# The last batch's output stored by pairs of units, from the ring of output buffers

## The chip, the cores and the metric

One core of one Trainium2 chip. The metric is the device time of one launch in microseconds, as the median of several runs; the profile is of one such execution, and its span is 1.7 to 2.5 us shorter than the time of that run. The records call an execution slow when it is over 1.5% above the fastest of its kernel. Ratios and differences are of fast runs alone.

## The reference

Attention through 32 inducing points, twice, and then a feed-forward layer with GELU over all tokens:

```python
B, N, m, C = (4, 12480, 32, 128)          # x: [4, 12480, 128] float32
def mab(q, kv):
    s = scale * (q @ kv.transpose(0, 2, 1))
    a = softmax(s)                        # with 1e-9 added to the sum
    return a @ kv
h = mab(inducing, x)                      # 32 x 128 per batch
y = mab(x, h).reshape(49920, 128)
out = gelu(y @ w_in) @ w_out              # 128 -> 2048 -> 128, float32 [49920, 128]
```

The input and the output are 25.6 MB each. That is what the kernel has to move, whatever else it does.

## The kernel before

Of the engines, PE multiplies matrices, DVE, ACT and POOL work on elements, and SP issues stores; 16 DMA engines move data between HBM and SBUF. A store is issued when SP hands it to its DMA queue, and it has landed when a semaphore tells that all its parts are written.

Each batch is cut into six units of 2048 tokens and a tail of 192. The first pass (A) loads x, transposes it and gathers the 32 inducing points. A short chain then makes one small matrix per batch. The second pass (B) makes the outputs unit by unit: four matmuls per unit leave 128 x 512 values each in PSUM, and DVE, or ACT, or ACT followed by POOL, scales them into a buffer in SBUF. SP stores from there. Loads are issued by POOL (the first by SP) and, where POOL issues them, converted to 16 bits on the way; stores are issued by SP.

```python
XBUFS = 6          # ring of input buffers, 8 KB a partition each (32 x 128 of 16 bits)
OBUFS = 3          # ring of output buffers, 16 KB a partition each (32 x 128 of 32 bits)
APART = 3          # from this batch on, each unit is stored alone
SPENT = (B - 3, 2) # this pair is written over a transposed input that is no longer read
...
class Unit:
    ...
        self.pair = idx // 2                                  # two units share a pair
        self.c_pair = 0 if self.tail else 16 * (idx % 2)      # this unit's half of it
...
    def b_inverse(bt, u):
        ...                       # reciprocal of the sums, then the choice of buffer
        if u.tail:
            o = sb.tile([TP, 2, 128], FP32, tag="ot", bufs=2)
        elif u.b >= APART:        # an input buffer, read as 32 bits: 16 x 128
            o = sb.tile([128, 32, 128], FP16, tag="xh", bufs=XBUFS)
            ...
        else:
            if u.first:
                if spent(u):
                    ...
                else:
                    pair = sb.tile([128, 32, 128], FP32, tag="o", bufs=OBUFS)
                bt.live[("pair", u.pair)] = pair
            o = bt.live[("pair", u.pair)][:, u.c_pair : u.c_pair + 16, :]
...
    def b_store(bt, u, alone):
        if alone:
            c0, c1, o = u.c_pair, u.c_pair + u.nc, bt.live[("o", u.idx)]
        else:
            c0, c1, o = 0, u.held, bt.live[("pair", u.pair)]
        nc.sync.dma_start(out=u.rows_of(out)[:, c0:c1, :], in_=o)
...
        alone = u.tail or u.b >= APART
        ...
        if u.last or alone:       # a pair is stored when its second unit is scaled
            stored = plan.add(key(6), {"SP": 0.4}, ...)
```

The order of all instructions comes from a list scheduler that the kernel runs while it is built. It knows the rings and an assumed duration of each piece; the order is then pinned for each engine.

Of the kernel before, what the change touches and what calls it, by code (L numbers as in the profile page):

```python
# [31 lines left out]
LOAD_US = 2.43  # L32
STORE_US = 2.47
LEAD = (0, 0, 0, 0)
APART = 3
SPENT = (B - 3, 2)
LANDED_US = 1.1
FIRST_US = {"POOL": 1.3, "SP": 0.8}
# [210 lines left out]
def kernel(  # L249
# [409 lines left out]
    def b_inverse(bt, u):  # L659
# [4 lines left out]
        if u.tail:  # L664
            o = sb.tile([TP, 2, 128], FP32, tag="ot", bufs=2)
        elif u.b >= APART:
            o = sb.tile([128, 32, 128], FP16, tag="xh", bufs=XBUFS)
# [214 lines left out]
    for k, u in enumerate(order):  # L882
# [24 lines left out]
        )  # L907
        alone = u.tail or u.b >= APART
        if alone:
# [382 lines left out]
```

## Time and profile before

| | |
|---|---|
| time | 133.07 us, median of 3 (132.73 to 133.23) |
| span of the profile | 131.5 us |
| PE, DVE, ACT, POOL busy | 77%, 70%, 59%, 50% of the span |
| HBM traffic | 27.67 MB read, 25.56 MB written, 405 GB/s over the span |

The page's DMA row gives, for each fortieth of the span, the share of time in which the 16 DMA engines moved something, in tenths; the GB/s row gives what they moved, counted in what was written. A load that halves the data on its way therefore counts half. Behind these rows stand the packet records of the trace: for each row of a transfer its start, duration, size and queue, but not its engine. How many of the 16 engines are busy is counted from them.

### The profile page before, as it was taken

The page shows a single profiled execution, that of the slowest core. Times are in us where ns is not written, and L with a number is a line of the kernel's source. Part 1 is how long each engine was busy: PE and PEld are TensorE (multiplying, and loading weights), DVE is VectorE, ACT ScalarE, POOL GpSimd, SP SyncE. Part 2 cuts the span into 40 slices and gives each one's busy share as a digit, 9 for nine tenths or more (in the row PEclk, how much of TensorE's full clock was granted, in tenths as well). Part 3 has the DMA queues.
Part 4 walks back from the last instruction along what each step waited for, and adds up shares of the span by engine and source line. Part 5 has one row for each costly group of instructions (what it writes and reads, how often), then busy time and mean ns, then how long its engine had stood idle before and what let it go on. Part 6 is the DMA issues. An engine that isn't in the chain of part 4 may idle for free. (4 is left out here: it accounts for less than half of the span.)

```text
span 131.5 us, 3505 instructions
## 1 busy us (share of the span) xinstructions
PE 101.8 (77%) x1365; PEld 60.0 (46%) x1365; DVE 91.9 (70%) x265; ACT 77.1 (59%) x177; POOL 65.6 (50%) x85
## 2 busy tenths in 40 slices
PE   0967789479999999999697699999999499781000
PEld 0255656278646557565362565735645312320000
DVE  1825447525899998999999367999899756997000
ACT  3006154426776879499787378889797457754000
POOL 7910131039634556894815367965269763483000
PEclk9999869855999999999999689999999856999555
DMA  5999999999999999999999999999999999999981
GB/s 152 298 228 209 217 198 219 218 214 222 214 209 214 214 229 339 306 387 368 322 304 339 277 251 297 316 401 411 439 425 415 419 444 419 411 426 424 431 349 43
DMA packets 5666, 40.17 MB, mean 305 GB/s; under 512 B 624, under 2 KB 1936, under 8 KB 2192
## 3 DMA queue, kind: packets, MB, share of 16 engines
q0 software_dynamic: 2848, 13.30, 49.9%
q1 hardware_dynamic: 2752, 26.61, 48.5%
q8 instruction: 11, 0.18, 0.5%
q10 hardware_dynamic: 48, 0.02, 0.1%
q14 instruction: 7, 0.06, 0.1%
HBM read 27.67 MB, written 25.56 MB: 405 GB/s over the span
## 5 line engine op out<-in xcount | busy, mean ns | idle before, releaser
L702 POOL TENSOR_TENSOR pair<-pair,rr 128x512 f32<-128x512 f32 x26 | 26.8, 1043 | 19.6 <-ACT pair L365 16.7
L686 PE MATMUL at<-q,e 128*128 128x512 f16 (+1 forms) x104 | 33.7, 391 | 3.6 <-DVE xT L363 1.2
L377 PE MATMUL tr<-identity_h,xh 128*128 128x128 f16 x392 | 32.7, 244 | 3.1 <-DMA xh<-in_x_dram 3.1
L377 PEld LDWEIGHTS <-xh 128*128 128x128 f16 x392 | 27.5, 111 | 9.2 <-DMA xh<-in_x_dram 4.2
L363 DVE COPY xT<-tr 128x1024 f16<-128x1024 f16 (+1 forms) x36 | 22.7, 646 | 10.1 <-PE tr L377 9.6
L365 ACT ACTIVATE xT<-tr 128x1024 f16<-128x1024 f16 (+1 forms) x16 | 15.7, 980 | 18.6 <-PE tr L377 18.5
L717 DVE TENSOR_TENSOR pair<-at,rr 128x512 f32<-128x512 f32 x36 | 23.3, 676 | 1.1 <-PE at L686 0.4
L287 POOL DMA_DIRECT2D xh<-in_x_dram x15 | 8.3, 555 | 21.3 <-DMA xh<-in_x_dram 10.5
L403 ACT ACTIVATE e<-s 128x512 f16<-128x512 f32 (+1 forms) x28 | 15.3, 546 | 5.7 <-PE s L391 5.4
L638 ACT ACTIVATE e<-s 128x512 f16<-128x512 f32 (+1 forms) x28 | 14.9, 562 | 3.4 <-PE s L626 1.8
L365 ACT ACTIVATE pair<-at 128x512 f32<-128x512 f32 x26 | 15.7, 602 | 1.1 <-PE at L686 1.0
L417 DVE STREAM_TRANSPOSE e1t<-e 128x256 int32<-128x256 int32 (+1 forms) x28 | 11.1, 399 | 3.4 <-ACT e L403 3.3
L686 PEld LDWEIGHTS <-e 128*128 128x128 f16 (+1 forms) x104 | 8.7, 103 | 10.2 <-issue 6.7
L425 PE MATMUL hun<-xh,e1t 128*32 128x128 f16 x392 | 10.8, 226 | 3.1 <-DVE e1t L417 3.0
L572 POOL TENSOR_TENSOR pt<-pt 128x512 f32<-128x512 f32 (+4 forms) x20 | 12.0, 602 | 2.1 <-DVE rr L661 0.7
L717 DVE TENSOR_TENSOR o<-at,rr 128x512 f32<-128x512 f32 (+1 forms) x19 | 10.5, 579 | 2.9 <-PE at L686 2.5
L391 PE MATMUL s<-xT,indT 128*32 128x512 f16 (+1 forms) x108 | 10.5, 379 | 1.4 <-DVE xT L363 0.8
L425 PEld LDWEIGHTS <-e1t 128*32 128x32 f16 x392 | 6.4, 98 | 8.9 <-DVE e1t L417 6.5
L626 PE MATMUL s<-xT,hT 128*32 128x512 f16 (+1 forms) x100 | 10.0, 407 | 0.5 <-DVE rr L661 0.5
L702 POOL TENSOR_TENSOR o<-o,rr 128x512 f32<-128x512 f32 x7 | 7.3, 1041 | 5.7 <-ACT o L365 3.3
L650 PEld LDWEIGHTS <-e 128*128 128x128 f16 (+1 forms) x104 | 5.7, 99 | 4.8 <-issue 1.9
L650 PE MATMUL r<-strand,e 128*128 128x4 f16 (+1 forms) x104 | 6.7, 168 | 0.2 <-ACT e L403 0.2
(76 smaller groups left out, 102.0 us busy)
## 6 DMA issues: line engine op xcount, KB each, us to landing
out_dram<-pair SPq DMA_DIRECT2D x8, 2048.0 KB, 15.0
xh<-in_x_dram POOLq DMA_DIRECT2D x11, 1024.0 KB, 28.2
out_dram<-o SPq DMA_DIRECT2D x6, 1024.0 KB, 8.8
out_dram<-spent SPq DMA_DIRECT2D x1, 2048.0 KB, 16.1
x_first<-in_x_dram SPq DMA_DIRECT2D x1, 1024.0 KB, 5.2
xh<-in_x_dram POOLq DMA_DIRECT2D x1, 512.0 KB, 6.9
w_in_h<-in_moe_w_in_dram POOLq DMA_DIRECT2D x1, 512.0 KB, 17.2
w_out_h<-in_moe_w_out_dram POOLq DMA_DIRECT2D x1, 512.0 KB, 19.2
```

The source lines that it names most:

```text
L363: nc.vector.tensor_copy(out=out, in_=in_)
L365: nc.scalar.activation(out=out, in_=in_, func=AF.Copy)
L377: nc.tensor.transpose(tr[:, c - c0, : u.p], xh[: u.p, c, :], identity_h[: u.p, : u.p])
L403: nc.scalar.activation(out=e1[: u.p, : u.nc // 2, :, :], in_=s1[: u.p, : u.nc, :].rearrange("r (a b) i -> r a i b", b=2), func=AF.Exp, sca ...
L417: nc.vector.transpose(out=pairs(e1t)[: u.p, :n], in_=pairs(e1)[: u.p, :n])
L425: nc.tensor.matmul(bt.hun[32 * j : 32 * j + 32, :], e1t[: u.p, c // 2, :, c % 2], xh[: u.p, c, :], start=u.idx == 0 and c < 4, stop=c + 4 ...
L572: nc.gpsimd.tensor_tensor(out=bt.pt[:, :, :, :half], in0=bt.pt[:, :, :, :half], in1=bt.pt[:, :, :, half : 2 * half], op=ALU.add,)
L638: nc.scalar.activation(out=e2[: u.rows, : u.cols], in_=s2[: u.rows, : u.cols], func=AF.Exp, scale=SCALE,)
L650: nc.tensor.matmul(r2[: u.p, ci, : u.nj], e2[: u.rows, ci * u.p : (ci + 1) * u.p], strand[: u.rows, : u.nj], start=True, stop=True,)
L686: nc.tensor.matmul(at[: u.p, : u.nj, :], e2[: u.rows, ci * u.p : (ci + 1) * u.p], bt.q[: u.rows, : u.nj, :], start=True, stop=True,)
L702: nc.gpsimd.tensor_tensor(out=part, in0=part, in1=rr2[: u.p, ci, : u.nj].unsqueeze(2).broadcast_to([u.p, u.nj, 128]), op=ALU.mult,)
L717: nc.vector.tensor_tensor(out=ov[: u.p, ci, :, :], in0=at[: u.p, : u.nj, :], in1=rr2[: u.p, ci, : u.nj].unsqueeze(2).broadcast_to([u.p, u. ...
```

## The change

The intent is to store all full units in the same way: pairs in rows of 16 KB a partition, from the ring of three output buffers, the last batch's too.

```diff
-APART = 3
+APART = 4
```

With four batches, numbered 0 to 3, no unit is then stored alone but the tails. In the last batch three stores of 2 MB take the place of six of 1 MB.

## The prediction

> **What bounds the kernel now.** I read the page's slices first, then the busy times by stretch, then the chain that ended last, then the DMA issues, and last the store line itself in narrow stretches. The slices and three rows of the page:
>
> ```profile
> span 131.5 us, 3505 instructions
> DVE  1825447525899998999999367999899756997000
> DMA  5999999999999999999999999999999999999981
> GB/s 152 298 228 209 217 198 219 218 214 222 214 209 214 214 229 339 306 387 368 322 304 339 277 251 297 316 401 411 439 425 415 419 444 419 411 426 424 431 349 43
> ...
> out_dram<-pair SPq DMA_DIRECT2D x8, 2048.0 KB, 15.0
> out_dram<-o SPq DMA_DIRECT2D x6, 1024.0 KB, 8.8
> ```
>
> One slice is 3.29 us. The compute engines are finished three slices before the end, the DMA engines almost at it, and from the 27th slice on the GB/s row stays at 401 to 444. So the last 43 us are one unbroken stream of output. The busy times by stretch say the same, with the row length in them (columns: stretch, length, busy time of PE, PEld, DVE, ACT, POOL, clock, DMA share, GB/s):
>
> ```profile
> 90.00:100.00 10.00, 9.70 (x117) 5.09 (x117) 9.46 (x26) 8.87 (x26) 5.64 (x6) 1.00 1.01 425
> 100.00:110.00 10.00, 7.81 (x74) 3.16 (x74) 7.09 (x21) 5.38 (x14) 6.99 (x10) 0.70 1.00 424
> 110.00:120.00 10.00, 7.47 (x48) 2.79 (x44) 9.36 (x32) 7.04 (x18) 5.80 (x6) 0.96 1.00 421
> ```
>
> Until about 112 us this stream is pairs of units (2 MB, rows of 16 KB); after it, single units (1 MB, rows of 8 KB). 425, 424 and 421 GB/s: the row length hardly shows.
>
> The chain of waits stops in the checks at the end of compute, because the profile cannot follow a landing back to its store. It is still useful, since its last piece gives the end of compute:
>
> ```profile
> 119.86 0.60 DVE hit L438 x8
> ...
> 120.95 0.14 DVE failed L979
> ```
>
> Compute is over at 121.1, 10.4 us before the end. What ends the run is the landing of the last stores. The store line in stretches that hold one issue each:
>
> ```profile
> L729 SPq DMA_DIRECT2D out_dram<-o x1: 333/333/333, 108.6 to 108.6; - x1
> DMA to landing us min/median/max: 9.1/9.1/9.1
> L729 SPq DMA_DIRECT2D out_dram<-o x1: 332/332/332, 111.8 to 111.8; - x1
> DMA to landing us min/median/max: 8.5/8.5/8.5
> L729 SPq DMA_DIRECT2D out_dram<-o x1: 332/332/332, 116.7 to 116.7; - x1
> DMA to landing us min/median/max: 8.5/8.5/8.5
> L729 SPq DMA_DIRECT2D out_dram<-o x1: 332/332/332, 119.8 to 119.8; - x1
> DMA to landing us min/median/max: 11.3/11.3/11.3
> L729 SPq DMA_DIRECT2D out_dram<-o x1: 1105/1105/1105, 120.2 to 120.2; - x1
> DMA to landing us min/median/max: 11.1/11.1/11.1
> ```
>
> These are units 0, 1, 3 and 5 of the last batch and its tail. Each waits 8 to 11 us in the queue though it moves for 2.5 us only. The tail lands at 120.2 + 11.1 = 131.3, and the span is 131.5: the stores end the run. Unit 0 lands at 117.7, unit 1 at 120.3, unit 3 at 125.2, unit 5 at 131.1.
>
> **What the Trainium skill says.** Page "DMA: Bandwidth & Descriptors", section "Bandwidth" (Measured): a 16 MB transfer runs at 425 GB/s, 97% of peak; the trace agrees, with 421 to 425 here. Its section "Queues, rings and completion order" says that on each DMA engine the descriptors of a row are taken in ring order, and its section "Why a DMA increments its semaphore by 16 and not by 1" that a transfer has landed only when all its engines have. The trace agrees: stores land in order of issue, and the slowest engine's share decides. Its section "Latency and other measured facts" puts the first byte of this path at about 0.6 us. The trace's nearest case is the first load: 5.2 us from issue to landing for 1 MB on idle engines, of which some 2.5 are transfer, so 2.7 us of fixed cost at both ends. I use the trace's number.
>
> **The change, part by part.** One constant. In the last batch the six full units no longer take a buffer of 8 KB a partition each out of the ring of six input buffers; three pairs of units take 16 KB a partition each from the ring of three output buffers, as the pairs of the other batches do, and three stores of 2 MB take the place of six of 1 MB. Nothing else moves: matmuls, exponentials, scalings and bytes are the same.
>
> (1) Removed: three issues on SP, 3 x 0.33 = 1.0 us, on an engine that otherwise waits. Worth 0 on the end.
>
> (2) Bytes per second. 6 x 1.05 MB = 6.3 MB at 421 GB/s is 14.9 us, at 425 it is 14.8. The packets themselves say the same: in the trace's packet records a piece of 8 KB takes 309 to 324 ns on one DMA engine and one of 16 KB 611 to 624. Worth 0 to -0.1 us. The longer rows buy nothing measurable.
>
> (3) Later issues. A pair can go only when its second unit is scaled. With the compute of before, the three issues stand where those of units 1, 3 and 5 stand now: 111.8, 116.7 and 119.8. The last one is unmoved, and so is the tail's. What matters is whether the queue runs dry before the first two. Ahead of pair 0 lie the last pair and the tail of batch 2. Their issues, 101.8 and 103.6, are 13.0 and 11.5 from landing, so the queue ahead is empty at 114.8 to 115.1 (slowest engine). Pair 0 issued at 111.8 has 3.3 us until then, against 2.7 of fixed cost (part of it at the far end, so needed less): no gap on the slowest engine. On the faster ones there is a gap: in the packet records the engines finish the 16 KB rows of batch 2 between 112.5 and 114.3, and a store issued at 111.8 starts by my estimate at 113.2 (the first load's first packet came 1.4 us after its issue), perhaps up to 2 us later under load. Faster engines have slack, since at the end they finish between 127.4 and 129.6, and the slowest only at 131.
>
> (4) Pair 0 then lands at 115.1 + 2 x 2.45 = 120.0 (2.45 us a MB from units 1 and 3: 125.2 - 120.3 = 4.9 for two). Pair 1 is issued at 116.7, again 3.3 us ahead: same margin. It lands at 124.9. Pair 2 is issued at 119.8 with 5 us in hand and lands at about 129.8; the same sum for before would give 115.1 + 6 x 2.45 = 129.8 against 131.1 measured, because the last stores on the slowest engine are slower (units 3 to 5 take 5.9 us and not 4.9; at 126.4 to 127 instruction fetches run there). I carry this 1.3 over: 131.1, tail 131.3. So +0 from this step, and +0.5 if the start under load takes 3.5 us instead of 1.4.
>
> (5) The output ring. Three buffers: pair 0 reuses that of batch 2's first pair, pair 1 the second's, pair 2 the third's. Those land at 104.6, 109.7 and 114.8 (issues 91.5, 98.5 and 101.8 plus 13.1, 11.1 and 13.0). First writes into units 0, 2 and 4 in the timeline of before: 106.1, 111.5 and about 116.1. Slack 1.5, 1.8 and 1.3 us: no wait if the order stays. In before these units wait for nothing either, because the input buffers have long been free.
>
> (6) The order of instructions comes from a list scheduler in the kernel, which will now see these three rings as taken and may put pieces of the last batch in another order. I cannot work that out from a profile; I allow 0 to +1 us, mean +0.3.
>
> Sum: -0.1 + 0 to 0.5 + 0.3, so 133.07 + 0.4, rounded: 133.5.
>
> **The rivals.** (a) Longer rows are faster and the change gains: for it speaks only 425 against 421; by 1% of 14.9 us it would make 132.9. Against it, the packet times. (b) The queue runs dry twice because a pair goes out later by one unit (3.2 us at pair 0: 108.6 to 111.8; 2.4 us at pair 1: 114.3 to 116.7), and nothing hides it: margin 0.6 us lost plus, say, 1.5 us of gap: 134.5 to 135. For it speaks that the backlog, 8 to 11 us for single units, shrinks to some 3 us. (c) The output ring becomes a wait: if the scheduler or slower landings push pair 1 or 2 back, each us of wait delays the issue and, since the margin of step 3 is spent, the end: 135 to 137. Against it: 1.3 to 1.8 us of slack at each of the three. (d) Compute gains by the freed input ring: no, nothing loads any more, 0.
>
> **Range and chances.** Most of the weight lies on steps 3 to 5, between 133.0 and 134.0; rival b and c make the upper tail. Range 132.7 to 135.2. Faster by over 2% (under 130.4) would need the stream to move 20% faster or start earlier: 1%. Slower by over 2% (over 135.7) needs rival c, or b in full: 8%. Within 2%: 91%.
>
> **What would show it.** Steps right: the GB/s row from 90 to 127 us without a slice under 400; three pair issues near 111.8, 116.7 and 119.8; waits of SP still on the scaling engines; landing of pair 0 about 8 us after issue, of pair 2 about 11; the span about 131.5 to 132. Step 3 wrong: a dip in the slices near 114 and 119, and landing of pair 0 after 120.5. Step 5 wrong: scalings of the last batch that wait for the landing of an output store. Step 6 wrong: the last scaling ends clearly later than 119.7. Step 2 wrong: over 430 GB/s after 115 us, and an earlier end.

## The result, and the profile after

| | before | after |
|---|---|---|
| time, median of 5 | 133.07 us (132.63 to 133.23) | 132.99 us (132.93 to 133.16) |
| span of the profile | 131.5 us | 131.1 us |

The ratio is 1.0004, with a 95% interval of 0.9982 to 1.0027: the same. (A ratio here is the mean time of one kernel's fast runs over the mean of the other's in the same rounds, so it is not quite the ratio of the medians.)

The stretches of after, with the same columns as those of before in the prediction (length, busy time of PE, PEld, DVE, ACT, POOL, clock, DMA share, GB/s):

```profile
90.00:100.00 10.00, 9.94 (x134) 5.36 (x131) 9.49 (x22) 7.94 (x20) 6.31 (x7) 1.00 1.01 427
100.00:110.00 10.00, 7.81 (x58) 2.71 (x55) 6.80 (x22) 5.52 (x13) 5.89 (x8) 0.66 1.01 429
110.00:120.00 10.00, 6.18 (x38) 2.34 (x37) 8.37 (x31) 7.00 (x20) 5.20 (x5) 0.95 1.01 429
```

The stream of stores has no hole. From 110 to 120 us it is 429 GB/s where it was 421; the 427 and 429 of the stretches ahead, whose rows are 16 KB in both kernels, differ by 2 and 5 from the 425 and 424 of before, so much of that is not the change; and from 116 to 126 us, where before moves single units alone, it is 429 against 426. In the packet records, all 16 engines are busy from 5 us to 126.7 us in both kernels.

The three pair stores of the last batch and its tail, one answer of the store line per issue (time of issue, and time from there to landing):

```profile
L729 SPq DMA_DIRECT2D out_dram<-pair x1: 332/332/332, 109.9 to 109.9; - x1
DMA to landing us min/median/max: 10.0/10.0/10.0
L729 SPq DMA_DIRECT2D out_dram<-pair x1: 332/332/332, 114.9 to 114.9; - x1
DMA to landing us min/median/max: 10.0/10.0/10.0
L729 SPq DMA_DIRECT2D out_dram<-pair x1: 333/333/333, 119.1 to 119.1; - x1
DMA to landing us min/median/max: 11.6/11.6/11.6
L729 SPq DMA_DIRECT2D out_dram<-o x1: 723/723/723, 119.5 to 119.5; - x1
DMA to landing us min/median/max: 11.4/11.4/11.4
```

So the pairs land at 119.9, 124.9 and 130.7 and the tail at 130.9. Units 1, 3 and 5 of before landed at 120.3, 125.2 and 131.1. The landings agree within half a microsecond, though these pairs were issued up to 2 us earlier than those units. The issues moved; the landings did not.

One thing is new. The chain that ended last goes through the landing of a store in after (start, length, what):

```profile
100.11 14.76 DMA out_dram<-pair
114.88 0.03 issue
114.90 0.05 DVEq L717
114.95 0.04 issue
115.00 0.69 DVE pair L717
```

The first scaling into the last batch's third pair waits until the store that empties its buffer has landed, at 114.9. The timeline has the same for the second pair:

```profile
110.12 0.60 ACT L365 ACTIVATE pair<-at 128x512 f32<-128x512 f32 x1 [0.35 <-DMA out_dram<-pair]
```

The ring of output buffers has become a wait in this execution, then, and the stream of stores has no hole from it. (In a second execution of the same program, below, the buffers came free 1.1 to 1.8 us before they were written.) The experiments ask why the time stands still: is it because nothing in the change has a cost, or because a gain and a loss cancel?

### The profile page after: what moved, and what is told of

Its sections match the earlier page's. It is cut to its first block, busy times and chain, and to the rows that moved or that the text cites. A ratio compares the mean times of both kernels' runs of the same rounds, so it can differ in the third digit from the quotient of the medians.

```text
span 131.1 us, 3497 instructions
## 1 busy us (share of the span) xinstructions
PE 100.7 (77%) x1365; PEld 59.2 (45%) x1365; DVE 91.6 (70%) x264; ACT 77.8 (59%) x181; POOL 65.5 (50%) x85
## 5 line engine op out<-in xcount | busy, mean ns | idle before, releaser
L702 POOL TENSOR_TENSOR pair<-pair,rr 128x512 f32<-128x512 f32 x33 | 34.1, 1040 | 26.5 <-ACT pair L365 20.4
L686 PE MATMUL at<-q,e 128*128 128x512 f16 (+1 forms) x104 | 33.1, 385 | 4.4 <-DVE xT L363 1.2
L717 DVE TENSOR_TENSOR pair<-at,rr 128x512 f32<-128x512 f32 x49 | 31.9, 679 | 4.7 <-PE at L686 2.9
L377 PE MATMUL tr<-identity_h,xh 128*128 128x128 f16 x392 | 31.4, 238 | 2.5 <-DMA xh<-in_x_dram 2.4
L377 PEld LDWEIGHTS <-xh 128*128 128x128 f16 x392 | 26.3, 108 | 8.8 <-DMA xh<-in_x_dram 3.8
L365 ACT ACTIVATE pair<-at 128x512 f32<-128x512 f32 x33 | 19.9, 603 | 5.9 <-PE at L686 4.4
L638 ACT ACTIVATE e<-s 128x512 f16<-128x512 f32 (+1 forms) x28 | 14.9, 562 | 3.2 <-PE s L626 1.8
L425 PE MATMUL hun<-xh,e1t 128*32 128x128 f16 x392 | 11.3, 235 | 3.0 <-DVE e1t L417 3.0
L710 ACT ACTIVATE pair<-at,rr 128x128 f32<-128x128 f32 x24 | 6.9, 382 | 0.9 <-DVE rr L661 0.9
L391 PEld LDWEIGHTS <-indT 128*32 128x32 f16 x108 | 3.5, 94 | 6.1 <-issue 3.2
```

The source lines that it names most:

```text
L365: nc.scalar.activation(out=out, in_=in_, func=AF.Copy)
L377: nc.tensor.transpose(tr[:, c - c0, : u.p], xh[: u.p, c, :], identity_h[: u.p, : u.p])
L391: nc.tensor.matmul(s1[32 * j : 32 * j + 32, : u.nc, :], indT, xT[:, :, 32 * j : 32 * j + 32], start=True, stop=True,)
L425: nc.tensor.matmul(bt.hun[32 * j : 32 * j + 32, :], e1t[: u.p, c // 2, :, c % 2], xh[: u.p, c, :], start=u.idx == 0 and c < 4, stop=c + 4 ...
L638: nc.scalar.activation(out=e2[: u.rows, : u.cols], in_=s2[: u.rows, : u.cols], func=AF.Exp, scale=SCALE,)
L686: nc.tensor.matmul(at[: u.p, : u.nj, :], e2[: u.rows, ci * u.p : (ci + 1) * u.p], bt.q[: u.rows, : u.nj, :], start=True, stop=True,)
```

## The experiments

The theory: the DMA engines are full to the end, so bytes set the time; the change keeps the bytes, and its later issues and ring waits stay inside what the queue ahead still holds. The rivals: (A) long rows gain and later issues lose, and the two cancel; (B) the ring costs time; (C) the stores are hidden whatever one does, so that something else ends the run. All edits are to the kernel after unless it is said. The edits are shown shortened. Each run was timed in 5 rounds beside the kernel before, whose median was 133.02 us beside four runs (each unit alone, two halves, the hold that was none, rows of 2 KB), 133.03 beside four (the two reversed orders, the store left out at the end, rows of 8 KB everywhere) and 133.28 beside the other four. Executions called slow: one of six with the second pair first, two of six with the third pair first and with either store left out.

### Same buffers, each unit stored as soon as it is done

```diff
+        if u.b == B - 1 and not u.tail:        # the unit's own half of the pair
+            c0, c1, o = u.c_pair, u.c_pair + u.nc, bt.live[("o", u.idx)]
         nc.sync.dma_start(out=u.rows_of(out)[:, c0:c1, :], in_=o)
...
-        if u.last or alone:
+        if u.last or alone or halved:          # halved: a full unit of the last batch
```

> The last batch writes into the pair buffers of the output ring, as in the kernel after, but each unit is stored alone as soon as it is done: 1 MB, rows of 8 KB. Theory (the 16 DMA engines are full to the end, bytes set the time, and both issue times leave the queue filled): 133.0, within 0.3 of before and after. Rival A (longer rows gain and later issues lose, and the two cancel): earlier issues without the ring of input buffers give nothing else, so 133.0 to 133.1 as well, but then the next run must be slower. Rival B (the ring of three costs time): 133.5 or more.

Measured: 132.99 us, ratio 0.9996 (0.9958 to 1.0034). Output buffers in place of input buffers, with the rows of before and each unit issued by itself (in this profile up to 1.7 us earlier than in before), make no difference.

### Same moment, short rows

```diff
-        nc.sync.dma_start(out=u.rows_of(out)[:, c0:c1, :], in_=o)
+        # last batch, full units: rows of 8 KB, two stores at the moment of one
+        for c in range(c0, c1, 16):
+            nc.sync.dma_start(out=u.rows_of(out)[:, c:c+16, :], in_=o[:, c-c0:c-c0+16, :])
```

> As after, at the same moment, but each pair of the last batch goes as two stores of 1 MB with rows of 8 KB. Only the row length differs from after. Theory: 133.0 to 133.2 (the packet records give 616 ns for 16 KB and 2 x 311 for twice 8 KB, 1% of 14.9 us = 0.15 us). Rival A (cancelling): 133.4 or more, as the gain of the long rows is gone and the later issue stays.

Measured: 133.06 us, ratio 0.9994 (0.9959 to 1.0029). The run is not slower than after, so there is no gain of the long rows for a loss to cancel, within the 0.3 to 0.4% that the interval allows. Rival A falls for a gain of 0.4 us or more; a smaller one this run can't exclude. The packet records of this run give 311 ns for a piece of 8 KB in the last stretch, those of after 616 for 16 KB: 1% between them, some 0.15 us of the 14.9, below what these runs can see.

### A hold that was none

```diff
+        if u.b == B - 1 and u.pair < 2 and not u.tail:
+            held.append((dst, o))
+            if u.pair < 1:
+                return
+            for dst, src in held:              # first pair, then second pair
+                nc.sync.dma_start(out=dst, in_=src)
+            return
```

> As after, but the store of the last batch's first pair is held back until its second pair is done, so its issue moves from about 109.9 to about 114.9 us, when the queue ahead of it empties (landing of the tail before it at 115.1 in the profile of after). Theory (issue times are free only as long as the queue ahead is not empty, with some 2.7 us of fixed cost per store): a gap of 1.4 to 2.5 us in the stream, 134.4 to 135.5. Rival C (stores at the end are hidden whatever their issue): 133.0.

Measured: 132.83 us, ratio 1.0000 (0.9948 to 1.0052). This is no evidence against the theory, because the edit did not do what it was meant to. The trace has the first pair's issue at 111.8, 5.0 us ahead of the second's at 116.8. Emitting an issue later in the program doesn't delay it: the two issues stand in SP's list in the same order, and each waits only for the writers of its own buffer. In the trace SP, DVE, ACT, POOL and PE do the same work in the same order as in after, so the run is a repetition of it.

As a repetition it is useful. In this execution the last pair of the batch before was issued at 102.1 us, in the profile of after at 100.1. Compute was 2 us later, and the spans are 131.0 and 131.1. The end does not follow compute. Nor is there a wait for the ring here: its buffers came free at 105.0, 109.9 and 114.7 us and were first written at 106.2, 111.6 and 115.8.

### The hold, made real: the second pair's store first

```diff
-            for dst, src in held:
+            for dst, src in [late[-1]] + late[:-1]:   # second pair, then first
```

> The hold that the third run was meant to be: in the last batch the store of the second pair is issued first and that of the first pair right after it, so that nothing of this batch is issued before about 114.9 to 116.8 us, while the queue ahead empties at about 115.1. Theory (an issue is free as long as it comes some 2 us before the queue ahead is empty): a gap of 1.4 to 3 us in the stream, 134.4 to 136. Rival C (issue times at the end are hidden anyway): 133.0.

Measured: 135.50 us, ratio 1.0191 (1.0160 to 1.0221): 2.5 us slower, inside what was expected. Rival C falls. The rows of its page:

```profile
DMA  4999999999999999999999999999999998499992
GB/s 125 302 226 209 223 197 215 221 211 216 216 221 204 226 231 331 328 402 348 300 334 327 258 250 322 339 427 417 432 425 422 432 427 338 168 393 462 395 415 103
```

The hole is in the 34th to 36th slices (338, 168 and 393 GB/s where 427 stands ahead and 462 behind). The queue ahead, issued at 101.9 and 13.2 us from landing, was empty at 115.1, and the first store of this batch was issued at 115.1:

```profile
L734 SPq DMA_DIRECT2D out_dram<-pair x1: 332/332/332, 115.1 to 115.1; - x1
DMA to landing us min/median/max: 6.3/6.3/6.3
```

On an empty queue 2 MB take 6.3 us from issue to landing. Of these 4.9 are eight pieces of 616 ns on each engine. In the packet records the first piece starts 0.83 us after the issue and all 16 engines work 0.98 us after it. The first engines had run out of pieces at 111.9, over 3 us ahead of the landing at 115.1.

### One step further: the third pair's store first

```diff
-        if u.b == B - 1 and u.pair < 2 and not u.tail:
+        if u.b == B - 1 and u.pair < 3 and not u.tail:
...
-            if len(late) < 2:
+            if len(late) < 3:          # then the order is pair 2, 0, 1
```

> The same one step further: the third pair's store goes first, then the first's and the second's, so nothing of the last batch is issued before about 119 to 120 us. Theory: the engines stand idle from about 115 to 121, +5.5 to +7, so 138.5 to 140. Rival C: 133.0.

Measured: 140.58 us, ratio 1.0534 (1.0490 to 1.0579), 7.1 us slower, just over the upper edge of what was expected.

```profile
DMA  5999999999999999999999999999999960199993
GB/s 152 284 222 221 203 205 222 221 216 214 212 218 216 235 297 337 338 413 302 318 347 236 279 309 335 370 430 432 423 425 418 442 284 5 76 380 449 430 399 128
```

The engines do almost nothing for two slices (3.45 us each here) and two thirds of the usual in the one ahead. In the packet records the mean engine stands idle for 7.4 us between 105 and 126 us, 2.8 us in the run above and 0.0 in after. Each microsecond of hole is about a microsecond of time: 2.8 gives 2.5, 7.4 gives 7.1. The first piece of the late store starts 0.83 us after the issue.

### One pair's store left out, at the end and at the start

Both give a wrong result: 2.1 MB of the output are never written.

```diff
+        if u.b == B - 1 and u.pair == 1 and not u.tail:    # first run
+        if u.b == 0 and u.pair == 0:                       # second run
+            return
         nc.sync.dma_start(out=u.rows_of(out)[:, c0:c1, :], in_=o)
```

> Wrong on purpose: as after, but the store of the last batch's second pair is left out, 2.1 MB less; nothing else changes. Theory (bytes over full engines set the end): 4.9 us less, 128.1. If compute or the closing waits set the end: 133.0, or a smaller gain (compute ends 11 us before the end, so up to 11 us can show).

Measured: 129.86 us, ratio 0.9693 (0.9647 to 0.9738), 4.1 us less (the four fast executions took 128.46 to 129.88). It is short of 4.9, as its rows tell: with the second pair gone, the queue was empty before the third was issued, at 120.3, and a slice has 97 GB/s. Its holes come to 3.2 us for the mean engine; part of that comes back at the end, where the engines finish closer together (1.2 us of idle time of the mean engine, in after 3.0).

```profile
DMA  4999999999999999999999999999999999998295
GB/s 141 301 219 220 215 205 208 222 210 218 218 207 215 223 213 305 315 352 394 342 295 331 343 230 270 318 320 402 453 410 429 420 410 446 430 395 348 97 410 205
```

> Wrong on purpose: as after, but the store of the first batch's first pair is left out, 2.1 MB less at 45 us instead of at the end. If full DMA engines bind the whole run (the DMA row of the page is at 9 from the second slice on): 4.9 us less, as far as compute can follow, 128 to 129. If only the last 43 us are bound by the engines and the middle by compute (PE 9.7 to 9.9 of 10 us there): 0 to 2 us less, 131 to 133.

Measured: 128.80 us, ratio 0.9662 (0.9615 to 0.9709), 4.5 us less (fast executions 128.12 to 129.29). A store left out at 45 us is worth as much as one left out at the end, within the intervals. So the engines bind from 45 us at the latest and not only in the last 43 us. The buffer that the missing store frees is hardly the cause: in after no wait for the landing of an output store stands in the list of waits ahead of 100 us. The DMA row of before is full from its second slice on; the GB/s row hides it, because loads count half. For the time ahead of 45 us no run tests it.

### Two output buffers in place of three

Before and after, both with `OBUFS = 2`, and one more order for the reciprocals that two buffers need:

```diff
-OBUFS = 3
+OBUFS = 2
...
-            [p] if u.first else [p, p_r2],
+            [p] if u.idx == 0 else [p, p_r2],
```

(Without the second edit, both read unset data; a ring of four doesn't fit into SBUF.)

> The kernel before with two output buffers in place of three (and the reciprocal of each tail ordered behind the units before it, which two buffers need to be free of a read of unset data). Reference for the next run: the first three batches wait more for landings, 133.5 to 138.

> The kernel after with the same two output buffers, to enlarge the wait of the last batch for the ring. If a ring wait of the last batch reaches the end once it is longer than what the queue holds: the first pair starts when the pair but one before it has landed (about 111 us), its issue comes after the queue ahead is empty, and the third pair starts when the first has landed: 3 to 6 us more than the run before. If ring waits are always hidden: equal to it.

Measured: 143.47 us for before and 143.48 for after, ratios to the kernel before with three buffers 1.0764 (1.0713 to 1.0815) and 1.0789 (1.0739 to 1.0839), so equal within intervals of half a per cent; a cost of a microsecond would not show. The first expectation was too low: before loses 10 us with two buffers, 5 more than the most I had thought. And the 3 to 6 us that the ring might cost the last batch are not there. Its waits are (after with two buffers, from 95 to 130 us; columns: us in total, times, longest):

```profile
DVE pair L717 <- DMA out_dram<-pair: 4.5, 2, 2.5
ACT pair L365 <- DMA out_dram<-pair: 3.7, 2, 2.2
```

The last batch's pairs are issued at 123.3, 128.5 and 133.9 in this trace, 5.2 to 5.5 us apart, and each pair needs 4.9 in the engines. A pair that waits for the landing of the last but one is computed while the last one moves, which hides most of the wait, but not all of it. The GB/s rows of before and of after, both with two buffers (the last batch fills slices 35 to 40):

```profile
GB/s 187 254 221 208 206 203 229 220 208 213 213 224 210 203 323 346 383 354 267 213 327 339 276 311 430 430 168 374 260 150 449 154 444 260 411 411 423 423 418 119
GB/s 181 257 225 211 207 200 216 220 225 218 213 211 208 227 308 348 393 340 259 248 308 333 268 348 426 431 69 445 183 222 370 153 445 252 370 445 370 370 440 190
```

After has three dips to 370 where before has 411 and more. In the packet records these are holes at 123.5, 129.0 and 134.2 us, one ahead of each pair, of 0.6, 0.3 and 0.5 us for the mean engine; before has none there. At the end after's engines finish closer together (1.2 us of idle time and not 2.1), and the medians don't differ. So rival B falls for the change itself: with three buffers there is no hole. With two buffers a wait of 4.5 us leaves 1.4 us of holes in this execution, and whether these cost time the intervals can't tell. Buffers do matter in the batches ahead of it, where holes of up to a slice stand in the rows of both kernels.

### Shorter rows everywhere

```diff
+        # all batches: 16 (rows of 8 KB) or 4 (rows of 2 KB) in place of 32
+        for c in range(c0, c1, 4):
+            nc.sync.dma_start(out=u.rows_of(out)[:, c:c+4, :], in_=o[:, c-c0:c-c0+4, :])
```

> As after, but every pair of all four batches goes as eight stores with rows of 2 KB. From the packet times (1 KB 46 ns, 8 KB 309 ns: 9 ns each and 36.6 ns a KB) a row of 2 KB takes 83 ns against 77 for an eighth of 16 KB, 8% more on 25.2 MB of stores, 59 us of all engines. If the DMA engines bind the whole run: +4.7 us, 137.7. If they bind only the last 43 us, some 18 MB: +3.4, 136.4. If row length is without any cost: 133.0.

Measured: 141.24 us, ratio 1.0625 (1.0575 to 1.0675), 8.2 us slower. The piece of 2 KB takes 84 ns (median), as worked out, so the expectation failed elsewhere. Where, the waits show:

```profile
POOL pair L702 <- DMA out_dram<-pair: 18.2, 4, 14.9
ACT pair L365 <- DMA out_dram<-pair: 15.3, 2, 12.9
DVE pair L717 <- DMA out_dram<-pair: 13.3, 1, 13.3
```

DVE scaled nothing for 13 us, up to 75.1 us, because no output buffer came free. The packet records tell why. They give the rows that each queue began, and the stores' share of the engines' time, in a stretch in which both queues had work:

| rows of the stores | one row | one row of a load | rows of stores and of loads, 60 to 68 us | stores' share there | if rows alternate |
|---|---|---|---|---|---|
| 16 KB (after) | 616 ns | 625 ns | 100 and 107 | 50% | 50% |
| 8 KB (run below) | 311 ns | 625 ns | 140 and 137 | 35% | 33% |
| 2 KB | 84 ns | 625 ns | 192 and 181 | 14% | 12% |

The Trainium skill's page "DMA: Bandwidth & Descriptors", section "Queues, rings and completion order", says that each DMA engine takes turns between the queues by packets. The records agree on the turns, and a turn is one row: about as many rows of each queue, and nearly every end of a row coincides, within 24 ns, with the start of a row of the other queue (8 KB run), while rows of the same queue show no such excess. So a queue with short rows gets little of the engines while the other has work. A row of 2 KB in place of 16 costs only 9% by itself; against a queue of long rows it costs the stores most of their share.

> As after, but every pair of all four batches goes as two stores with rows of 8 KB, issued at the same moment. If the length of a row matters only by its own packet time (616 ns for 16 KB against 2 x 311): +1% of the 59 us that all engines spend on stores, 133.0 to 133.6. If, as the run with 2 KB rows suggests, engines alternate packet by packet between the loads' queue (625 ns a packet) and the stores' queue, then while loads run the stores get 311 of 936, a third, where they had half: stores of the first two batches fall behind, output buffers come free later, 133.6 to 136, and the waits of POOL and DVE for landings appear in the middle of the run.

Measured: 134.32 us, ratio 1.0086 (1.0063 to 1.0110), 1.1 us slower, and of the waits that this theory expects those of DVE and ACT are there, up to 72.7 us (POOL has none):

```profile
DVE pair L717 <- DMA out_dram<-pair: 3.5, 1, 3.5
ACT pair L365 <- DMA out_dram<-pair: 3.2, 1, 3.2
```

So long rows are worth 1% of this kernel in the first three batches, where loads run beside the stores (to 88 us in after, 82 in this run), and nothing that these runs can see in the last, where the loads are over. The kernel before already had them where they pay.

### An attempt at a better version

```diff
+        if u.b == B - 1 and u.pair == 2 and not u.tail:
+            dst = u.rows_of(out)
+            nc.sync.dma_start(out=dst[:120, :, :], in_=o[:120, :, :])
+            nc.sync.dma_start(out=dst[120:, :, :], in_=o[120:, :, :])
+            return
```

> An attempt to beat both. In the profiles 15 engines finish the last pair between 127 and 129.6 us, one alone at 130.5 to 131. As after, but the third pair of the last batch goes as two stores: 120 partitions (by the Trainium skill, page DMA: Bandwidth & Descriptors, section Why a DMA increments its semaphore by 16 and not by 1, a shape of 120 runs on the lowest 15 engines) and 8 partitions (8 engines, one row of 16 KB more each). If the slow engine is the one left out: about 1.2 us less, 131.8. If it is another: +0.3 to +0.6, as that one gets a row more or nothing changes, 133.0 to 133.6.

Measured: 136.27 us, ratio 1.0218 (1.0175 to 1.0262), 2.9 us slower, worse than either expectation. In the packet records one engine is without work from 122.5 us on, so the engine that was left out was an early one. The pieces of 16 KB that start after 122.5 us, most of them of this store, take 893 ns on average, some up to 1.9 us; those between 112 and 122.5 us take 615. Why these pieces are longer no run here shows. No version was found that beats both kernels; what remains at the end, 3 us in which the engines finish one after another, stays open.

## Why the prediction was right

It said 133.5, within 132.7 to 135.2, and the same by 91%; measured was 132.99. The mechanism was the right one: full DMA engines, and later issues hidden by the queue ahead. The 0.4 us above the kernel before were allowances of steps 3 and 6 that were not needed. By its steps:

1. Fewer issues on SP, worth nothing: right, as part of a time that did not move (the two halves have these issues back, at the same time).
2. Bytes per second, 0 to -0.1 us: right. The run with two halves is the same within its interval.
3. Later issues inside the queue ahead: the verdict is right, two sizes were not. The start of a store was put at 1.4 us after its issue, or 3.5 under load; on an empty queue it is 0.83, and also in the repetition of after, where the pair was issued at 111.84 while most engines still worked. The fixed cost of both ends was put at 2.7 us, from a first load; for a store of 2 MB it is 6.3 - 4.9 = 1.4. That first load was misread: its pieces run from 1.28 to 5.13 us in the records, so it started 1.0 us after its issue at 0.26, and 3.85 and not 2.5 of its 5.2 us are transfer, which leaves 1.35 for both ends. The gap that the step saw on the faster engines is 0.1 us in the repetition and not there in after. The margin was thus larger than thought, and the +0 to 0.5 us allowed for it were not needed. That the margin is real, and that its loss costs what the hole is long, the reversed stores show (+2.5 and +7.1 us).
4. Landings at 120.0, 124.9 and 131.1: measured 119.9, 124.9 and 130.7. The 1.3 us that were carried over for the slower last pair show again, as 0.8 to 0.9 us (130.7 - 124.9 = 5.8, against 4.9 or 5.0 for the pairs before).
5. "No wait if the order stays": wrong for the profiled execution, right for its repetition. In the profile of after, buffers came free at 105.2, 110.0 and 114.9 and the first writes are at 105.3, 110.1 and 115.0. The landings stood where they had been, within 0.6 us; compute was 1.7 us earlier in this execution (the last pair of the third batch went at 100.1 and not at 101.8). The slack of 1.3 to 1.8 us had been read from one execution. In the repetition, with compute 2 us later, it is 1.1 to 1.8 us again. That the wait costs nothing was right as to the end, but for a reason the prediction didn't give: where compute is early enough to wait, the queue ahead still holds enough.
6. The scheduler's order, +0.3 us: it changed a little (on DVE one reciprocal moved ahead of two scalings, and ACT took one scaling alone that DVE had done), and the last scaling ended at 119.1, not later than the 119.9 of before. The allowance was not needed.

Its opening held the run bound by the DMA engines for the last 43 us. That was too narrow. The store left out shows that they bind from 45 us at the latest.

Of its rivals, (a) falls with the two halves for a gain of 0.4 us or more, (b) describes a real cost that this change doesn't reach, and (c) a wait that comes in one of two executions and is hidden.

## What to carry to other kernels

When the last stores wait 8 to 11 us in the queue, the moment of issue and the buffer they leave from are free until the queue ahead runs empty; compare each issue plus the start of a transfer (0.8 to 1.0 us here) with the moment at which the engines run out of pieces, and beyond that count a microsecond of hole as about one of time. That moment is earlier than the landing of the store ahead: by 0.5 us with two buffers, and for the first engine by over 3 us with the second pair first. Look for the benefit of long rows where two queues share the engines, not where one runs alone. Count holes from the packet records; samples at whole microseconds can miss them. Read slack from several executions, and check that an edit meant to delay an issue does delay it in the trace.

## What the Trainium skill lacked or had wrong

- Page "DMA: Bandwidth & Descriptors", section "Latency and other measured facts", puts the first byte of the path that SP's transfers take at about 0.6 us. Here the first piece of a store on an empty queue starts 0.83 us after the issue, and all engines work 0.98 us after it.
- The same page, section "Bandwidth" (Measured), has 341 GB/s for 1 MB and 425 for 16 MB, both for loads issued from GpSimd. It has no figure for stores that follow one another in a queue: those of 1 MB run at 426 GB/s here and those of 2 MB at 429 (before and after, 116 to 126 us), and the time is the same (133.07 and 132.99 us).
- The same page, section "Queues, rings and completion order", names the turns between queues, with packets of some 9 to 17 descriptors. In the packet records here a turn is one row. The page does not say that the length of a row then sets a queue's share: 50%, 35% and 14% of the engines' time for stores in rows of 16, 8 and 2 KB beside loads of 625 ns a row; the shorter rows cost 1.1 and 8.2 us.
- No page has what a store over 120 partitions costs: once it ran, pieces of 16 KB took 893 ns on average, where they took 615 ahead of it.
